# The o matmuls of nine MLP units by Strassen's method: seven products of halves, with the sums on VectorE

## The chip, the cores and the metric

The kernel runs on one core of one Trainium2 chip. The metric is the device time of one execution in microseconds. Before the change it was 677.96 us (median of three runs, 677.47 to 679.17).

## What is computed

A gated linear recurrence (4 batches, 8 heads, 768 tokens, head size 48) gives 3072 tokens of 384 features. They go through an MLP with 2048 hidden features and the activation h · sigmoid(1.702 h).

```python
# q, k, v, f_logit: (4, 8, 768, 48) float32;  w_in (384, 2048), w_out (2048, 384): float64
f = 1.0 / (1.0 + np.exp(-f_logit))
for t in range(S):
    state = f[:, :, t, :, None] * state + np.einsum('bhd,bhe->bhde', k[:, :, t], v[:, :, t])
    y[:, :, t] = np.einsum('bhd,bhde->bhe', q[:, :, t], state)
x = y.transpose(0, 2, 1, 3).reshape(B * S, H * D)      # (3072, 384)
h = x @ w_in
g = h * (1.0 / (1.0 + np.exp(-1.702 * h)))
out = (g @ w_out).astype(np.float32)
```

The kernel computes in float32. The weights arrive as float64 and are turned into float32 by VectorE, a piece at a time (`convert`), so the first MLP units have to follow the arrival of the weights.

## The kernel before

Tokens are taken in 12 units of 256 (`NALL = 12`, `U = 256`). For each there is an attention unit (scores, masks, state, y) and an MLP unit. Units 0 to 2 do their MLP in quarters of the hidden features, as the weights come. Units 3 to 11 do it whole: 16 blocks of 128 hidden features (`NFF = 16`), four of them to a g tile (`FG = 4`).

```python
    P, G, U = 128, 128, 256;  NK = 3;  NFF = 16;  FG = 4;  DM = 384
    wp = ...tile_pool(name="wp", bufs=2)      # "bits": 3 buffers, "a": 4 (conversion of weights)
    mlp = ...tile_pool(name="mlp", bufs=2)
    ps = ...tile_pool(name="ps", bufs=1, space=PSUM)   # sc: 2 banks, y: 2 banks, "mm": 4 buffers of a bank
    ctx.enter_context(tc.manual_schedule(engines={mybir.EngineType.PE}))   # TensorE runs in program order
    ...
    def mlp_h(n, ffs, g):
        def one(ff, c):
            if c == 0:
                if ff % FG == 0:
                    g[ff // FG] = mlp.tile([P, FG, width(n)], F32, tag="g", ..., bufs=6)
                t["ph"] = ps.tile([P, width(n)], F32, tag="mm", ..., bufs=4)
            nc.tensor.matmul(ph, lhsT=w_in[:, c, ff * P:(ff + 1) * P], rhs=xTs[n][:, c, :],       # L619: h
                             start=(c == 0), stop=(c == NK - 1))
            if c == NK - 1:
                nc.scalar.activation(sg, ph, AF.Sigmoid, scale=1.702)                              # L624
                nc.vector.tensor_tensor(g[ff // FG][:, ff % FG, :], ph, sg, ALU.mult)              # L625
                ...                       # the last unit: one token more, its sum on VectorE (L631, L633)

    def mlp_o(n, ffs, g, done):
        def one(tt, ff):
            if ff == ffs[0]:
                t["po"] = ps.tile([P, DM], F32, tag="mm", ..., bufs=4)
            nc.tensor.matmul(t["po"], lhsT=g[ff // FG][:, ff % FG, tt * P:(tt + 1) * P],           # L645: o
                             rhs=w_out[:, ff, :], start=(ff == ffs[0]), stop=(ff == ffs[-1]))
            if ff == ffs[-1]:
                done(tt, t["po"])

    def mlp_unit(n):                      # units 3 to 11
        def done(tt, po):
            ...
            nc.scalar.copy(o, po)                                                                  # L664
            store(n, tt, o)
```

The matmuls of the MLP are a list, `fill`. `merge(n, fill, columns, share)` emits the parts of attention unit n on TensorE and puts a share of `fill`, counted in moving columns, behind each of them. In the steady part (merges 4 to 11) one attention unit goes with one MLP unit's worth of columns; what is left runs at the end without attention.

```python
    UNIT = NFF * NK * U + U // P * NFF * DM
    ...
    fill_order.close()                    # from here the scheduler orders all engines but TensorE
    for n in range(3, NALL):
        fill += mlp_unit(n)
    for n in range(4, NALL):
        merge(n, fill, UNIT, steady)
    for _, emit, _ in fill:
        emit()
```

Of attention these steps matter here. `scores` are matmuls into `sc` (L383). VectorE multiplies X by the gates' products for the next level (`promote`, L438), and ScalarE copies the keys and queries out of X (`set_aside`, Kc and Qc, L422); the next scores read these copies. VectorE takes the scores out under a mask (A, L409), and TensorE adds A · v to y (L447). VectorE turns q, k and f from the loaded layout (STREAM_TRANSPOSE, L326), once each for a unit. The state goes step by step on VectorE (st, L539 and L542) from scores of k and v (L522), and TensorE then adds the state's part to y (L562). `tkn` (L504) are transposes of k by TensorE.

Of the kernel before, what the change touches and what calls it, by code (L numbers as in the profile page):

```python
# [9 lines left out]
F32 = mybir.dt.float32  # L10
I32 = mybir.dt.int32
U32 = mybir.dt.uint32
AF = mybir.ActivationFunctionType
ALU = mybir.AluOpType
# [9 lines left out]
def kernel(  # L24
# [7 lines left out]
    moe_w_out: bass.AP,  # L32
    out: bass.AP,
):

# [19 lines left out]
    nc = tc.nc  # L57
    B, H, S, D = q.shape
    DM = H * D
    DFF = moe_w_in.shape[1]  # L60
    P = 128
    C = 64
    G = 128
    U = 256
# [7 lines left out]
    NK = DM // P  # L72
    NFF = DFF // P
    FG = 4
    PAIRS_AHEAD = 3
# [9 lines left out]
    wp = ctx.enter_context(tc.tile_pool(name="wp", bufs=2))  # L85
    mlp = ctx.enter_context(tc.tile_pool(name="mlp", bufs=2))
    ps = ctx.enter_context(tc.tile_pool(name="ps", bufs=1, space=bass.MemoryType.PSUM))
# [43 lines left out]
    X = const.tile([P, 3, NX], F32, name="X")  # L131
# [8 lines left out]
    w_out = const.tile([P, NFF, DM], F32, name="w_out")  # L140
# [7 lines left out]
    pieces, pairs = [], []  # L148
    for r in range(NGR):
        ffs = range(r * FG, (r + 1) * FG)  # L150
        for ff in ffs[::2]:
            f = slice(ff * P, (ff + 2) * P)
# [77 lines left out]
    def convert():  # L230

        if state["begin"] < len(pairs) and len(todo) <= NOP:
            begin_pair(state["begin"])
            state["begin"] += 1
        if todo and todo[0]:
            todo.pop(0)()
        if todo and todo[0] is None:
            todo.pop(0)
            state["done"] += 2
            fetch_weights()  # L240
# [360 lines left out]
        return (begin_f, begin, begin_k, begin_gates), parts  # L601


    xTs = {}

    def width(n):

        return U + (n == NALL - 1)

    def mlp_h(n, ffs, g):  # L610
        t = {}

        def one(ff, c):
            if c == 0:
                if ff % FG == 0:
                    g[ff // FG] = mlp.tile([P, FG, width(n)], F32, tag="g", name=f"g_{n}_{ff}", bufs=6)
                t["ph"] = ps.tile([P, width(n)], F32, tag="mm", name=f"h_{n}_{ff}", bufs=4)
            ph = t["ph"]
            nc.tensor.matmul(  # L619
                ph, lhsT=w_in[:, c, ff * P:(ff + 1) * P], rhs=xTs[n][:, c, :], start=(c == 0), stop=(c == NK - 1)  # L620
            )
            if c == NK - 1:
                sg = mlp.tile([P, width(n)], F32, tag="sg", name=f"sg_{n}_{ff}")
                nc.scalar.activation(sg, ph, AF.Sigmoid, scale=1.702)  # L624
                nc.vector.tensor_tensor(g[ff // FG][:, ff % FG, :], ph, sg, ALU.mult)  # L625
                if width(n) > U:

                    by = g[ff // FG][:, ff % FG, U:]
                    if ff == 0:
                        g["last"] = mlp.tile([P, 1, DM], F32, tag="sum", name="sum_last", bufs=3)  # L630
                        nc.vector.tensor_scalar(g["last"][:, 0], w_out[:, 0, :], by, None, op0=ALU.mult)  # L631
                    else:
                        nc.vector.scalar_tensor_tensor(  # L633
                            g["last"][:, 0], w_out[:, ff, :], by, g["last"][:, 0], op0=ALU.mult, op1=ALU.add
                        )
        return [(U, lambda ff=ff, c=c: one(ff, c), ff // FG * NPC + ff % FG + 1) for ff in ffs for c in range(NK)]

    def mlp_o(n, ffs, g, done):

        t = {}  # L640

        def one(tt, ff):
            if ff == ffs[0]:
                t["po"] = ps.tile([P, DM], F32, tag="mm", name=f"o_{n}_{tt}_{ff}", bufs=4)
            nc.tensor.matmul(  # L645
                t["po"], lhsT=g[ff // FG][:, ff % FG, tt * P:(tt + 1) * P], rhs=w_out[:, ff, :],
                start=(ff == ffs[0]), stop=(ff == ffs[-1]),
            )
            if ff == ffs[-1]:
                done(tt, t["po"])  # L650
        return [(DM, lambda tt=tt, ff=ff: one(tt, ff), (ff // FG + 1) * NPC) for tt in range(U // P) for ff in ffs]

    def store(n, tt, o):
        r0 = n * U + tt * P - 1
        nc.sync.dma_start(out=out[max(r0, 0):r0 + P, :], in_=o[1:] if r0 < 0 else o)

    def mlp_unit(n):
        g = {}

        def done(tt, po):  # L660
            if tt == 0:
                g["o"] = mlp.tile([P, U // P, DM], F32, tag="osb", name=f"osb_{n}", bufs=1)
            o = g["o"][:, tt]
            nc.scalar.copy(o, po)  # L664
            store(n, tt, o)

        def last_token():
            po = ps.tile([P, DM], F32, tag="mm", name="o_last", bufs=4)
            nc.tensor.matmul(po[:1], lhsT=ones, rhs=g["last"][:, 0], start=True, stop=True)
            nc.scalar.copy(g["last"][:1, 0], po[:1])  # L670
            nc.sync.dma_start(out=out[NALL * U - 1:, :], in_=g["last"][:1, 0])
        o = mlp_o(n, range(NFF), g, done)
        if width(n) > U:
            o.insert(NFF, (DM, last_token, 0))
        return mlp_h(n, range(NFF), g) + o

    sums = {}

# [25 lines left out]
    def parts_of(n):  # L704

        parts = list(units[n][1])
        _, inter = parts.pop()
        if n:
            kind, scores = parts[0]
            _, ahead = units[n - 1][1][-1]  # L710
            parts[0] = kind, lambda: (ahead(), scores())
        if n < N_TURN:

            def with_v(l):
                kind, fn = parts[l]
                return kind, lambda: (fn(), load_vl(n, l) if n == 0 or l else None)
            parts[:NL] = [with_v(l) for l in range(NL)]
        if n + 1 < NALL:
            begin_f, begin, begin_k, begin_gates = units[n + 1][0]
            i = len(parts)  # L720
            if n + 1 < N_FILL:

                parts.append(("K", lambda: (begin_k(), begin_gates(), load_vl(n + 1, 0) if n + 1 < N_TURN else None)))
                parts.insert(i - 4, ("B", begin))
                parts.insert(i - 5, ("B", begin_f))
            else:
                kind, states = parts.pop()
                parts += [("B", begin_k), (kind, lambda: (states(), begin_gates()))]
                parts.insert(i - 3, ("B", lambda: (begin_f(), begin())))
        else:  # L730
            parts.append(("W", inter))
        return parts

    def merge(n, fill, columns, share, pieces=0, hold=0, by=1.0):

        parts = parts_of(n)
        total = sum(share(kind) for kind, _ in parts)
        converting = {"W": 3, "T": 3, "B": 1} if n < N_FILL - 1 else {"W": 3, "V": 4, "S": 3, "T": 1, "B": 1}  # L740
        total_ops = sum(converting.get(kind, 0) for kind, _ in parts)
        held = sum(share(kind) for kind, _ in parts[:hold])
        at = at_ops = done = ops = 0
        for kind, fn in parts:
            ready = state["done"]
            fn()
            at += share(kind)
            at_ops += converting.get(kind, 0)
            n_ops = min(int(pieces * NOP * at_ops / (by * total_ops)), pieces * NOP) - ops
            ops += n_ops  # L750
            first, n_columns = done, max(0, columns * (at - held) / (total - held) - done)

            def some(end):
                nonlocal done
                while fill and done < end and fill[0][2] <= ready:
                    w, emit, _ = fill.pop(0)
                    emit()
                    done += w
            for i in range(n_ops):
                some(first + n_columns * i / n_ops)  # L760
                convert()
            some(first + n_columns)
# [4 lines left out]
    UNIT = NFF * NK * U + U // P * NFF * DM  # L767
# [13 lines left out]
    load_vn(1)  # L781
    fill = []
    merge(0, fill, 0, steady, 8)
    fill += mlp_blocks((0, 0)) + mlp_blocks((0, 1))
    merge(1, fill, UNIT // 2 - LAG // 2, steady, 10, hold=1)
    fill += mlp_blocks((1, 0), (1, 1)) + mlp_blocks((0, 2), (1, 2))
    merge(2, fill, UNIT, steady, 8)
    fill += mlp_blocks((2, 0), (2, 1)) + mlp_blocks((2, 2), (0, 3)) + mlp_blocks((1, 3), (2, 3))
    merge(3, fill, 3 * UNIT // 2 - LAG // 2, steady, 6, by=0.7)
    fill_order.close()  # L790
    for n in range(3, NALL):
        fill += mlp_unit(n)
    for n in range(4, NALL):
        merge(n, fill, UNIT, steady)
    for _, emit, _ in fill:
        emit()

# [28 lines left out]
```

## Time and profile before

| | |
|---|---|
| time | 677.96 us (677.47 to 679.17) |
| span of the profile | 674.0 us |
| busy: TensorE matmul, weight load | 652.6 us, 486.5 us |
| busy: VectorE, ScalarE, GpSimd | 378.4 us, 226.4 us, 50.3 us |
| granted TensorE clock, mean | 0.990 |
| DMA: data moved, mean rate | 67.62 MB, 100 GB/s |

Names in the profile: PE is TensorE's matmul, PEld its weight load, DVE VectorE, ACT ScalarE, POOL GpSimd, SP the engine that issues the DMAs. L645 is line 645 of the kernel. A row of the groups gives line, engine, operation, result<-operands, shape, count, then busy time and mean duration, then the idle time of the engine just before and what ended it. In the row of 40 slices a digit is the busy share in tenths. The chain that ended last follows the work back from the last instruction. The timeline lists instructions in order of time: start, length, engine, line, operation. Matmul records overlap their neighbours, since matmuls are pipelined, so their summed busy time counts more than the clock does.

### The profile page before, as it was taken

The page shows a single profiled execution, that of the slowest core. Times are in us where ns is not written, and L with a number is a line of the kernel's source. Part 1 is how long each engine was busy: PE and PEld are TensorE (multiplying, and loading weights), DVE is VectorE, ACT ScalarE, POOL GpSimd, SP SyncE. Part 2 cuts the span into 40 slices and gives each one's busy share as a digit, 9 for nine tenths or more (in the row PEclk, how much of TensorE's full clock was granted, in tenths as well). Part 3 has the DMA queues.
Part 4 walks back from the last instruction along what each step waited for, and adds up shares of the span by engine and source line. Part 5 has one row for each costly group of instructions (what it writes and reads, how often), then busy time and mean ns, then how long its engine had stood idle before and what let it go on. Part 6 is the DMA issues. An engine that isn't in the chain of part 4 may idle for free.

```text
span 674.0 us, 19354 instructions
## 1 busy us (share of the span) xinstructions
PE 652.6 (97%) x8514; PEld 486.5 (72%) x8514; DVE 378.4 (56%) x675; ACT 226.4 (34%) x459; POOL 50.3 (7%) x116
## 2 busy tenths in 40 slices
PE   5879999999999999999999999999999999999997
PEld 4656766757777886886886886876886786786774
DVE  3999877887666546545546546445446444430440
ACT  4564443343134233333333233233233233231210
POOL 3020020010002002002002002002002001000000
PEclk9789999999999999999999999999999999999999
DMA  8877973571063535415415415415414103001000
GB/s 193 226 192 193 240 160 89 152 185 37 24 159 107 154 66 149 109 38 148 115 33 152 110 37 148 113 37 144 115 37 115 37 24 84 15 1 36 13 1 24
DMA packets 67551, 67.62 MB, mean 100 GB/s; under 512 B 30410, under 2 KB 61290, under 8 KB 67466
## 3 DMA queue, kind: packets, MB, share of 16 engines
q1 hardware_dynamic: 67466, 66.38, 38.6%
q8 instruction: 67, 1.10, 0.7%
q14 instruction: 18, 0.15, 0.1%
HBM read 56.92 MB, written 8.65 MB: 97 GB/s over the span
## 4 chain that ended last, share of the span: by engine, by line
PE 89%; DVE 7%; ACT 2%; issue 1%; DMA 1%; SPq 0%; DVEq 0%; ACTq 0%
PE h L619 37%; PE o L645 35%; PE sc L383 5%; PE y L447 5%; PE t L338 2%; PE y L562 2%; PE tkn L504 1%; PE sc L522 1%; DVE s L218 1%; DVE A L409 1%; DMA xT<-yT 1%; PE tv L283 1%; ACT yT L570 1%; DVE X L436 1%; DVE X L438 1%
## 5 line engine op out<-in xcount | busy, mean ns | idle before, releaser
L619 PE MATMUL h<-xT,w_in 128*128 128x256 f32 (+1 forms) x1152 | 261.1, 382 | 1.1 <-DVE sum L690 0.8
L645 PE MATMUL o<-w_out,g 128*128 128x384 f32 x768 | 259.6, 491 | 0.9 <-DVE g L625 0.9
L619 PEld LDWEIGHTS h<-xT,w_in 128*128 128x128 f32 x1152 | 215.8, 190 | 36.8 <-issue 3.5
L645 PEld LDWEIGHTS o<-w_out,g 128*128 128x128 f32 x768 | 143.0, 190 | 94.5 <-issue 2.2
L625 DVE TENSOR_TENSOR g<-h,sg 128x256 f32<-128x256 f32 (+1 forms) x192 | 80.8, 422 | 133.1 <-ACT sg L624 132.6
L624 ACT ACTIVATE sg<-h 128x256 f32<-128x256 f32 (+1 forms) x192 | 73.2, 383 | 169.4 <-PE h L619 164.1
L422 ACT COPY Kc<-X 128x512 f32<-128x512 f32 x69 | 45.9, 666 | 123.7 <-DVE X L438 87.3
L438 DVE TENSOR_TENSOR X<-X,tot 128x1024 f32<-128x1024 f32 x45 | 55.2, 1226 | 54.8 <-PE sc L383 50.1
L409 DVE TENSOR_TENSOR A<-sc,masks 128x512 f32<-128x512 f32 x72 | 46.7, 679 | 0.0
L326 DVE STREAM_TRANSPOSE X<-raw 128x1024 f32<-128x1024 f32 x18 | 36.7, 2039 | 16.7 <-PE y L562 13.9
L447 PE MATMUL y<-A,vl 64*48 64x64 f32 x2304 | 41.7, 219 | 0.0
L447 PEld LDWEIGHTS y<-A,vl 64*48 64x48 f32 x2304 | 36.8, 122 | 5.3 <-issue 5.0
L375 POOL TENSOR_TENSOR tot<-F 128x512 f32<-128x512 f32 x12 | 12.5, 1039 | 340.5 <-DVE st L539 327.9
L383 PE MATMUL sc<-X,Kc 48*64 48x64 f32 x1344 | 29.0, 224 | 6.8 <-ACT Kc L422 4.6
L383 PEld LDWEIGHTS sc<-X,Kc 48*64 48x64 f32 x1344 | 24.6, 138 | 13.8 <-ACT Kc L422 7.2
L570 ACT COPY yT<-y 48x512 f32<-48x512 f32 x48 | 27.8, 580 | 20.0 <-PE y L562 19.4
L331 ACT ACTIVATE F<-F 128x1024 f32<-128x1024 f32 x9 | 9.5, 1057 | 49.0 <-DVE F L326 49.0
L375 POOL TENSOR_TENSOR tot<-tot 128x256 f32<-128x256 f32 (+4 forms) x60 | 23.7, 395 | 4.7
L542 DVE TENSOR_TENSOR st<-st,sc 128x192 f32<-128x192 f32 x44 | 15.6, 354 | 15.1 <-PE sc L522 13.7
L338 PE MATMUL t<-ident,raw 128*64 128x128 f32 x288 | 19.6, 298 | 4.4 <-DMA raw<-in_f_logit_dram 4.4
L338 PEld LDWEIGHTS t<-ident,raw 128*64 128x64 f32 x288 | 18.4, 153 | 7.0 <-issue 6.1
L664 ACT COPY osb<-o 128x384 f32<-128x384 f32 x18 | 8.6, 478 | 41.5 <-PE o L645 41.5
(66 smaller groups left out, 385.0 us busy)
## 6 DMA issues: line engine op xcount, KB each, us to landing
vl<-v_tok SPq DMA_DIRECT2D x60, 192.0 KB, 2.8
bits<-in_moe_w_out_dram SPq DMA_DIRECT2D x8, 768.0 KB, 9.8
bits<-in_moe_w_in_dram SPq DMA_DIRECT2D x8, 576.0 KB, 7.9
v_tok<-in_v_dram SPq DMA_DIRECT2D x10, 384.0 KB, 4.3
vn<-v_tok SPq DMA_DIRECT2D x10, 384.0 KB, 6.0
xT<-yT SPq DMA_DIRECT2D x24, 144.0 KB, 2.7
raw<-in_f_logit_dram SPq DMA_DIRECT2D x18, 192.0 KB, 3.9
raw<-in_q_dram SPq DMA_DIRECT2D x18, 192.0 KB, 3.1
```

The lines of the kernel that those rows point to most:

```text
L326: nc.vector.transpose(out.rearrange("p (a i j) -> p a j i", a=NP, j=R), raw[:, j].rearrange("p a (j d) -> p (a j) d", j=R)[:, :, :32],)
L338: nc.tensor.matmul(pt[h * HS:(h + 1) * HS, jj, :], lhsT=by_pair[j][:, h, x:x + HS], rhs=ident, start=True, stop=True)
L375: nc.gpsimd.tensor_tensor(tn, t2[:, :, 0], t2[:, :, 1], ALU.mult)
L383: nc.tensor.matmul(out[g * HS:(g + 1) * HS, h, a, :], lhsT=lhs(h, a * U + g * G), rhs=rhs(h, a * U + g * G), start=True, stop=True,)
L409: nc.vector.tensor_tensor(A[:, :, c:c + w].rearrange("p h (x t) -> p h x t", t=64), t["sc"][:, :, c:c + w].rearrange("p h (x t) -> p h x t ...
L422: nc.scalar.copy(c.rearrange("p (n m) -> p n m", m=m), X[:, j, :NA].rearrange("p (n two m) -> p n two m", two=2, m=m)[:, :, hf, :],)
L438: nc.vector.tensor_tensor(qk, qk, by, ALU.mult)
L447: nc.tensor.matmul(dst(h, g, a), lhsT=vls[n, u][g * 64:(g + 1) * 64, (2 * a + h) * D:(2 * a + h + 1) * D], rhs=A(h, g, a), start=(start an ...
L619: nc.tensor.matmul(ph, lhsT=w_in[:, c, ff * P:(ff + 1) * P], rhs=xTs[n][:, c, :], start=(c == 0), stop=(c == NK - 1))
L624: nc.scalar.activation(sg, ph, AF.Sigmoid, scale=1.702)
L625: nc.vector.tensor_tensor(g[ff // FG][:, ff % FG, :], ph, sg, ALU.mult)
L645: nc.tensor.matmul(t["po"], lhsT=g[ff // FG][:, ff % FG, tt * P:(tt + 1) * P], rhs=w_out[:, ff, :], start=(ff == ffs[0]), stop=(ff == ffs[ ...
```

## The change

The o of a unit is a product of two matrices that can be cut into halves each way. A is g: Aij has the tokens of half i (128) and the hidden blocks of half j (8 of 16). B is w_out: Bij has the hidden blocks of half i and the columns of half j (192 of 384). Eight products of halves make the result; by Strassen's method, in Winograd's form, seven do, with sums of halves:

- of B, once: T1 = B01 - B00, T2 = B11 - T1, T3 = B11 - B01, T4 = T2 - B10
- of A, in each unit: S1 = A10 + A11, S2 = S1 - A00, S3 = A00 - A10, S4 = A01 - S2
- products in TensorE's order: P1 = A00·B00, P4 = A11·T4, P2 = A01·B10, P6 = S2·T2, P5 = S1·T1, P7 = S3·T3, P3 = S4·B11
- result: out00 = P1 + P2; u2 = P1 + P6; u3 = u2 + P7; out10 = u3 - P4; out11 = u3 + P5; out01 = u2 + P5 + P3

Each product is 8 matmuls of 192 columns that add up in PSUM. There are four banks for them. X takes P1, and once that is copied out, P2 on top of it; Y takes P6 and then P7; Z takes P5 and then P3; W takes P4. VectorE makes the sums of A in SBUF: S1 in place of A10, S4 in place of A01, S2 and S3 in two more tiles of the pool of g. The sums of B use buffers of the conversion (`bits`, `a`) again. Units 3 to 11 are changed, units 0 to 2 are not. The aim is an eighth less of TensorE's work on o in these units.

```diff
+    HF, HC = NFF // 2, DM // 2
+    def quarter(w, i, j, ffs=slice(0, HF)):
+        return w[:, i * HF + ffs.start:i * HF + ffs.stop, j * HC:(j + 1) * HC]
+
+    def sums_of_b():                      # ten operations of VectorE, emitted two to a part of attention unit 4
+        for i in (1, 2, 3):
+            T[i] = wp.tile([P, 2 * DM * 2], I32, tag="bits", name=f"T{i}", bufs=PAIRS_AHEAD)
+            ...
+        t4 = [wp.tile([P, DM], F32, tag="a", name=f"T4_{f}", bufs=4)... for f in range(0, HF, n4)]
+        for x in h:                       # h: two halves of the 8 blocks
+            yield lambda x=x: sub(T[1][:, x], quarter(w_out, 0, 1, x), quarter(w_out, 0, 0, x))
+        for x in h:
+            yield lambda x=x: sub(T[2][:, x], quarter(w_out, 1, 1, x), T[1][:, x])
+        for x in h:
+            yield lambda x=x: sub(T[3][:, x], quarter(w_out, 1, 1, x), quarter(w_out, 0, 1, x))
+        for i in range(len(t4)):
+            yield lambda i=i, x=x: sub(t4[i], T[2][:, x], quarter(w_out, 1, 0, x))
+
+    def sums_of_a(n, g, b):               # after the four blocks of g tile b
+        if b < 2:
+            g["S", j] = mlp.tile([P, FG, width(n)], F32, tag="g", name=f"S_{n}_{j}", bufs=6)
+            tt(g["S", j][:, :, t1], g[j][:, :, t0], g[j][:, :, t1], ALU.subtract)
+        else:
+            tt(g[j][:, :, t1], g[j][:, :, t1], g[j + 2][:, :, t1], ALU.add)
+            tt(g["S", j][:, :, t0], g[j][:, :, t1], g[j][:, :, t0], ALU.subtract)
+
+    def last_sum(n, g):                   # S4, after P2 has read A01
+        for j in range(2):
+            nc.vector.tensor_tensor(g[j + 2][:, :, by], g[j + 2][:, :, by], g["S", j][:, :, by], ALU.subtract)
+
+    def mlp_o7(n, g):
+        def p1(): nc.scalar.copy(row("p1"), t["X"])
+        def p4(): nc.scalar.copy(row("p4"), t["W"])
+        def p2(): nc.scalar.copy(out_(0)[:, :HC], t["X"]); last_sum(n, g)
+        def p6(): nc.vector.tensor_tensor(row("u2"), t["p1"], t["Y"], ALU.add)
+        def p5(): nc.scalar.copy(row("p5"), t["Z"])
+        def p7():
+            nc.vector.tensor_tensor(row("u3"), t["p1"], t["Y"], ALU.add)
+            nc.vector.tensor_tensor(out_(1)[:, :HC], t["u3"], t["p4"], ALU.subtract)
+            nc.vector.tensor_tensor(out_(1)[:, HC:], t["u3"], t["p5"], ALU.add)
+            store(n, 1, out_(1))
+        def p3():
+            nc.vector.tensor_tensor(out_(0)[:, HC:], t["u2"], t["Z"], ALU.add)
+            store(n, 0, out_(0))
+        products = (
+            ("X", a(0, 0), b(0, 0), p1, True), ("W", a(1, 1), T_(4), p4, True), ("X", a(0, 1), b(1, 0), p2, False),
+            ("Y", s(0), T_(2), p6, True), ("Z", a(1, 0), T_(1), p5, True), ("Y", s(1), T_(3), p7, False),
+            ("Z", a(0, 1), b(1, 1), p3, False),
+        )
+        def one(bank, lhs, rhs, done, new, f):
+            if new and f == 0:
+                t[bank] = ps.tile([P, HC], F32, tag="mm", name=f"o_{n}_{bank}", bufs=4)
+            nc.tensor.matmul(t[bank], lhsT=lhs(f), rhs=rhs(f), start=(new and f == 0), stop=(f == HF - 1), ...)
+            if f == HF - 1:
+                done()
+        return [(HC, lambda p=p, f=f: one(*p, f), 0) for p in products for f in range(HF)]
 ...
     def mlp_unit(n):
-        o = mlp_o(n, range(NFF), g, done)
+        o = mlp_o7(n, g)
         if width(n) > U:
-            o.insert(NFF, (DM, last_token, 0))
-        return mlp_h(n, range(NFF), g) + o
+            o.insert(3 * HF, (DM, last_token, 0))
+        return mlp_h(n, range(NFF), g, True) + o       # mlp_h calls sums_of_a after each g tile
 ...
     for n in range(4, NALL):
-        merge(n, fill, UNIT, steady)
+        merge(n, fill, NFF * NK * U + 7 * HF * HC, steady, chores=list(sums_of_b()) if n == 4 else ())
```

More of the change, by code (lines that the diff above doesn't have):

```diff
@@ L601, in attention @@
         return (begin_f, begin, begin_k, begin_gates), parts
+    HF, HC = NFF // 2, DM // 2
+    T = {}
+    def quarter(w, i, j, ffs=slice(0, HF)):
[3 more added lines that the diff above has]
+            T[i] = wp.tile([P, 2 * DM * 2], I32, tag="bits", name=f"T{i}", bufs=PAIRS_AHEAD)
+            T[i] = T[i].bitcast(F32).rearrange("p (f e) -> p f e", f=HF)
+        n4 = DM // HC
+        t4 = [wp.tile([P, DM], F32, tag="a", name=f"T4_{f}", bufs=4).rearrange("p (f e) -> p f e", f=n4)
+              for f in range(0, HF, n4)]
+        T[4] = lambda f: t4[f // n4][:, f % n4]
+        sub = lambda *x: nc.vector.tensor_tensor(*x, ALU.subtract)
+        h = [slice(f, f + HF // 2) for f in (0, HF // 2)]
+        for x in h:
[5 more added lines that the diff above has]
+        for i in range(len(t4)):
+            x = slice(i * n4, (i + 1) * n4)
+            yield lambda i=i, x=x: sub(t4[i], T[2][:, x], quarter(w_out, 1, 0, x))
@@ new lines, in sums_of_a @@
+    def sums_of_a(n, g, b):
+        j = b % 2
+        t0, t1 = slice(0, G), slice(G, 2 * G)
+        tt = nc.vector.tensor_tensor
+        if b < 2:
[4 more added lines that the diff above has]
+            tt(g["S", j][:, :, t0], g[j][:, :, t1], g[j][:, :, t0], ALU.subtract)
@@ new lines, in last_sum, with out_, row, p1 @@
+    def last_sum(n, g):
+        for j in range(2):
+            by = slice(0, G)
+            nc.vector.tensor_tensor(g[j + 2][:, :, by], g[j + 2][:, :, by], g["S", j][:, :, by], ALU.subtract)
+    def mlp_o7(n, g):
+        a = lambda i, j: lambda f: g[j * 2 + f // FG][:, f % FG, i * G:(i + 1) * G]
+        s = lambda i: lambda f: g["S", f // FG][:, f % FG, i * G:(i + 1) * G]
+        b = lambda i, j: lambda f: quarter(w_out, i, j)[:, f]
+        T_ = lambda i: lambda f: T[i][:, f] if i < 4 else T[4](f)
+        t = {}
+        def out_(tt):
+            if "o" not in g:
+                g["o"] = mlp.tile([P, U // P, DM], F32, tag="osb", name=f"osb_{n}", bufs=1)
+            return g["o"][:, tt]
+        def row(name):
+            t[name] = mlp.tile([P, HC], F32, tag=name, name=f"{name}_{n}", bufs=1)
+            return t[name]
+        def p1():
+            nc.scalar.copy(row("p1"), t["X"])
+        def p4():
+            nc.scalar.copy(row("p4"), t["W"])
+        def p2():
+            nc.scalar.copy(out_(0)[:, :HC], t["X"])
+            last_sum(n, g)
+        def p6():
+            nc.vector.tensor_tensor(row("u2"), t["p1"], t["Y"], ALU.add)
+        def p5():
+            nc.scalar.copy(row("p5"), t["Z"])
+        def p7():
[14 more added lines that the diff above has]
+                t[bank] = ps.tile([P, HC], F32, tag="mm", name=f"o_{n}_{bank}", bufs=4)
+            nc.tensor.matmul(
+                t[bank], lhsT=lhs(f), rhs=rhs(f), start=(new and f == 0), stop=(f == HF - 1), skip_group_check=True,
+            )
+            if f == HF - 1:
+                done()
+        return [(HC, lambda p=p, f=f: one(*p, f), 0) for p in products for f in range(HF)]
@@ L608, in width, with mlp_h @@
         return U + (n == NALL - 1)
-    def mlp_h(n, ffs, g):
+    def mlp_h(n, ffs, g, sums=False):
         t = {}
@@ L625, in one @@
                 nc.vector.tensor_tensor(g[ff // FG][:, ff % FG, :], ph, sg, ALU.mult)
+                if sums and ff % FG == FG - 1:
+                    sums_of_a(n, g, ff // FG)
                 if width(n) > U:
@@ L658, in mlp_unit @@
         g = {}
[L660 to L665, printed above, removed]
         def last_token():
@@ L732, in parts_of, with merge @@
         return parts
-    def merge(n, fill, columns, share, pieces=0, hold=0, by=1.0):
+    def merge(n, fill, columns, share, pieces=0, hold=0, by=1.0, chores=()):
         parts = parts_of(n)
@@ L746, in merge @@
             fn()
+            for chore in chores[:2]:
+                chore()
+            chores = chores[2:]
             at += share(kind)
```

## The prediction

> **What bounds the kernel now.** I read the page's parts 1, 2 and 4 first.
>
> ```profile
> PE 652.6 (97%) x8514; PEld 486.5 (72%) x8514; DVE 378.4 (56%) x675; ACT 226.4 (34%) x459; POOL 50.3 (7%) x116
> ...
> PE   5879999999999999999999999999999999999997
> ...
> PE h L619 37%; PE o L645 35%; PE sc L383 5%; PE y L447 5%; PE t L338 2%; PE y L562 2%; PE tkn L504 1%; PE sc L522 1%; DVE s L218 1%; DVE A L409 1%; DMA xT<-yT 1%; PE tv L283 1%; ACT yT L570 1%; DVE X L436 1%; DVE X L438 1%
> ...
> L619 PE MATMUL h<-xT,w_in 128*128 128x256 f32 (+1 forms) x1152 | 261.1, 382 | 1.1 <-DVE sum L690 0.8
> L645 PE MATMUL o<-w_out,g 128*128 128x384 f32 x768 | 259.6, 491 | 0.9 <-DVE g L625 0.9
> ```
>
> TensorE is full from the fourth fortieth on, and h and o are 72% of the chain that ended last. Twelve units of 48 h matmuls and 32 o matmuls are 576 and 384, yet the groups count 1152 and 768: one fp32 matmul leaves two records. The mean durations (382, 491 ns) overlap, so they are no cost. The cost is the spacing, which the chain in order of time gives (start, length, line, records):
>
> ```profile
> 376.14 7.34 PE h L619 x34
> ...
> 648.90 10.32 PE o L645 x32
> ```
>
> 7.34 us / 34 = 215.9 ns for a record of 256 columns; 10.32 / 32 = 322.5 ns for 384. The slope is (322.5 - 215.9) / 128 = 0.833 ns a column, and 2.7 ns remain. In the steady part one period of one attention unit and one MLP unit takes 50.95 us (from the o group at 363.44 in that chain to its like at 414.39). There the list of waits has none on TensorE from 200 us on, and VectorE is half busy:
>
> ```profile
> 402.00:453.00 51.00, 51.00 (x682) 38.53 (x681) 26.18 (x39) 16.97 (x35) 4.29 (x8) 1.00 0.39 100
> ```
>
> (length; busy time and count of PE, PEld, DVE, ACT, POOL; clock; DMA.) So a column taken from TensorE is worth its full time, as long as nobody makes TensorE wait.
>
> **What the Trainium skill says.**
> - "FP8 and Floating Point Precision", TensorE Precision Notes: true fp32 takes four passes through the array. The trace agrees: two records of 0.833 ns a column, each two cycles of 2.4 GHz.
> - "TensorE: Matmul & The Clock Gate", LDWEIGHTS (loading the stationary operand): a load takes its columns / 1.2 ns whatever the rows, so 107 ns for 128 columns. The records of o and h say 190 ns. Which of the two counts is decided below, from the trace.
> - "VectorE: DVE Perf Modes", Mode 2×_2P: an fp32 tensor_tensor stays at one element a cycle. The trace agrees: 512 elements took 683 ns and 1024 took 1226 ns, 1.06 ns an element.
> - "PSUM — Partial Sum Buffer", PSUM bank collisions raise a hardware error: a matmul must not write a bank that another engine is reading. No run here shows a collision; but it is why a second product in a bank has to wait until the first has been copied out, and the change does that three times in a unit.
>
> **The change part by part.**
>
> *TensorE, removed and added.* Nine units (3 to 11) change. A unit's o had 2 x 16 matmuls of 384 columns, 64 records x 322.5 ns = 20.64 us. It gets 7 products x 8 matmuls of 192 columns, 112 records. By the line above a record is 215.9 - 64 x 0.833 = 162.6 ns, so 18.21 us. Saved: 2.43 us a unit, 21.8 us in all. The switches between the wide matmuls and the small attention ones are as many as before.
>
> *Does the weight load hide behind 162.6 ns?* Loads go from 64 to 112 a unit, + 9 x 48 x 190 ns = + 82 us of PEld busy, to about 569 us or 86%. If 190 ns were the least spacing, the gain would be gone. Where a tkn transpose (128 columns, one record) comes ahead of h, the timeline shows:
>
> ```profile
> 551.72 0.60 PE L504 MATMUL tkn<-ident,X 128*128 128x128 f32 x4
> 552.16 0.60 PE L619 MATMUL h<-xT,w_in 128*128 128x256 f32 x2
> ...
> 552.05 0.30 PEld L619 LDWEIGHTS h<-xT,w_in 128*128 128x128 f32 x2
> ```
>
> Two loads of 190 ns end 0.30 us after the first began, so they start 0.11 us apart, and the h matmul starts at 552.16, 0.11 us after the start of its own load. So 190 ns holds some 80 ns of latency, and a load occupies 110 ns at most. 162.6 ns is over that, and I count no load.
>
> *VectorE, added.* A unit: six sums of halves (512 elements, 0.68 us) and two last ones, 8 x 0.68 = 5.5 us; five adds of 192 columns out of PSUM at 0.354 us (the st<-st,sc row has that size) = 1.8 us. Together 7.2 us a unit. Once: sums of w_out, six of 768 elements (between 0.68 and 1.23 us, say 0.95) and four of 384 (0.55), 7.9 us. By amount it fits: 26.2 + 7.2 = 33.4 us of a period of 48.5. ScalarE loses two copies of 0.478 us and gets four of about 0.33 us. Nothing to see.
>
> *VectorE, where it lies.* This decides how much of the 21.8 us is kept. As built, each steady period runs on TensorE: y of the state (L562), scores, 1 matmul of P2, P6 (8), P5 (8), then P7, which adds into the bank of P6 and so waits until VectorE has read P6 for u2. On VectorE the order is: transposition of X, st, X multiply, two A, X multiply, last sum, u2. Before, the same stretch is (start, length):
>
> ```profile
> 413.53 2.05 DVE L326 STREAM_TRANSPOSE X<-raw 128x1024 f32<-128x1024 f32 x1 [2.14 <-PE y L562]
> 415.43 0.33 DVE L539 TENSOR_TENSOR st<-st,tot 128x192 f32<-128x192 f32 x1
> 415.69 1.21 DVE L438 TENSOR_TENSOR X<-X,tot 128x1024 f32<-128x1024 f32 x1
> 416.82 1.27 DVE L409 TENSOR_TENSOR A<-sc,masks 128x512 f32<-128x512 f32 x2
> 418.21 1.23 DVE L438 TENSOR_TENSOR X<-X,tot 128x1024 f32<-128x1024 f32 x1
> ...
> 414.32 9.30 PE L645 MATMUL o<-w_out,g 128*128 128x384 f32 x28
> ```
>
> VectorE ends at 419.44; with the last sum (0.68), u2 (0.35) and their gaps it has read P6 at about 420.6. TensorE, from 414.32, is through 17 matmuls of 2 x 162.6 ns at 419.85. So P7 waits about 0.75 us. This comes in seven periods (units 3 to 9; in the last attention unit the transposition is missing and VectorE is early): 7 x 0.75 = 5.3 us given back. After P7 there is air: u3 and the two sums end before the next scores, and the next Kc still comes over 2 us ahead of its scores.
>
> Other joints, by the same count: the S sums lie ahead of the state chain and end 0.3 us after its scores, with over 3 us before y needs the state. P4's last operand is ready about 4 us ahead. P2 and P3 have 2.6 us (one product) for ScalarE's copies of P1 and P5. In the last unit VectorE has 16 x (0.42 + 0.62) + 4.1 = 20.8 us beside 20.85 us of h, but P6 comes three products later. The end stays: an add of 0.35 us in place of a copy of 0.48 us, then the store.
>
> *Sums of w_out.* The scheduler puts the 7.9 us among the conversions of the last weights, at about 150 to 195 us, where VectorE is up to 73% busy. Most fits in its gaps; some g or sum that frees a bank will be late. I choose 1 us.
>
> Sum: 677.96 - 21.8 + 5.3 + 1.0 = 662.5 us.
>
> **The rivals.**
> - *Weight load is the bound.* At 190 ns a record: 112 x 0.190 = 21.28 us against 20.64, nine units cost 5.8 us, and the time is 684. The 190 ns rows speak for it, the loads 0.11 us apart against it; no 192-column fp32 matmul has run yet, so it isn't ruled out. A mild form, 5 ns more a record, costs 1008 x 5 ns = 5 us: 667.5.
> - *All of it is kept.* VectorE reads P6 in time and the w_out sums find gaps: 656.2. The order as built speaks against it.
> - *VectorE is late at more joints.* If each steady period waits 1.5 to 2 us in place of 0.75, the time is 668 to 671. For it: VectorE goes from 51% to about 68% of a period and executes in order, behind 2 us transposes. Against it: the margins above, mostly 2 us and more.
> - *g buffers run out* (six of a pool of six in a unit, four before). Each is read for the last time before the next unit's h of the same place is through, so I give it nothing.
>
> **Range and chances.** The mechanism spans 656 (all kept) to 671 (late at more joints); 0.75 us a period is a difference of two sums that may be off by half a microsecond, 3.5 us in all, and the 1 us may be 3. So 656.5 to 668.5. Faster by over 2% means under 664.4, only 1.9 us above my number: 0.66. Slower by over 2% needs the weight load and stalls together: 0.01. The rest, 0.33, is within 2%.
>
> **What would show it.** Right: o records of 192 columns some 163 ns apart; a steady period of about 49.3 us (50.95 - 2.43 + 0.75); one wait of TensorE's o on VectorE's u2 in a period, 0.5 to 1 us long; PEld near 569 us, DVE near 451 us (378 + 65 + 8). Wrong: o records 175 to 190 ns apart (weight load); a period of 48.5 us with no wait on u2; waits of sc on Kc, y on st or h on g in the steady part; more than 3 us of new waits between 150 and 230 us.

## The result and the profile after

The changed kernel took 661.47 us (median of four runs, 659.69 to 662.94) against 677.73 us of the kernel before beside it: a ratio of 0.9755, 95% interval 0.9723 to 0.9786. A second time, on its own (below), it was 0.9744, 0.9721 to 0.9766.

From the page of the changed kernel, the parts with busy time, slices, the chain's shares and the groups of o. Line numbers have moved: h is L727, the o of units 0 to 2 L755, the o of the seven products L704, with the bank in the name.

```profile
PE 632.1 (96%) x8946; PEld 542.3 (82%) x8946; DVE 443.9 (67%) x802; ACT 230.6 (35%) x477; POOL 54.0 (8%) x116
...
PE   6669989998999999999999999999999999999997
...
PE h L727 36%; PE o L755 7%; PE o_X L704 7%; PE o_Y L704 5%; PE o_Z L704 5%; PE sc L384 5%; PE y L448 4%; PE o_W L704 4%; DVE X L439 3%; PE t L339 2%; PE y L563 2%; DMA vn<-v_tok 1%; PE sc L523 1%; PE tkn L505 1%; DMA xT<-yT 1%
...
L704 PE MATMUL o_X<-w_out,g 128*128 128x192 f32 x288 | 53.8, 332 | 0.0
L704 PE MATMUL o_Y<-T,S 128*128 128x192 f32 x288 | 50.8, 329 | 1.3 <-DVE u L679 1.2
```

TensorE is still full, but VectorE has entered the chain: `X L439` rose from 1% to 3%, and one row of the seven products has idle time ahead of it, released by `u L679`. That is u2, the add that reads P6. The list of who waited for whom, for TensorE from 235 us to the end, has this line alone (total, times, longest):

```profile
PE o_Y L704 <- DVE u L679: 1.2, 4, 0.3
```

The wait comes six times, once in each of six periods; two of them are too short for this list, which takes idle times over 0.15 us. It is in these six periods, and in no other steady one, that the chain runs through VectorE. The chain in order of time shows the spacing and the period:

```profile
306.95 2.60 PE o_W L704 x16
...
351.03 1.62 PE o_X L704 x10
...
400.10 1.63 PE o_X L704 x10
```

2.60 us / 16 = 162.5 ns for a record of 192 columns; 162.6 was predicted. P1 comes every 49.07 us here, and 48.99 us in the mean of the six periods that have the wait. Before, it was 50.94.

The wait itself, in the timeline of the changed kernel, first TensorE, then VectorE:

```profile
411.64 0.59 PE L704 MATMUL o_X<-w_out,g 128*128 128x192 f32 x2
412.07 2.77 PE L704 MATMUL o_Y<-T,S 128*128 128x192 f32 x16
414.67 2.76 PE L704 MATMUL o_Z<-T,g 128*128 128x192 f32 x16
417.71 2.87 PE L704 MATMUL o_Y<-T,S 128*128 128x192 f32 x16 [0.27 <-DVE u L679]
...
413.03 1.22 DVE L439 TENSOR_TENSOR X<-X,tot 128x1024 f32<-128x1024 f32 x1
414.17 1.28 DVE L410 TENSOR_TENSOR A<-sc,masks 128x512 f32<-128x512 f32 x2
415.56 1.25 DVE L439 TENSOR_TENSOR X<-X,tot 128x1024 f32<-128x1024 f32 x1
416.70 0.69 DVE L650 TENSOR_TENSOR g<-g,S 128x512 f32<-128x512 f32 x1
417.31 0.35 DVE L679 TENSOR_TENSOR u<-p,o_Y 128x192 f32<-128x192 f32 x1
```

P7 (the second o_Y) starts at 417.71, right behind the end of u2 at 417.66. P6 takes 2.60 us from its first record to the first of P5 (412.07 to 414.67), P5 took 3.04. The list says 0.27 us only, because the last record before the wait is listed at 326 ns though the next could have come after 162.5.

### The profile page after: what moved, and what is told of

The parts are those of the page before. It is cut to its first block, busy times and chain, and to the rows that moved or that the text cites. A ratio compares the mean times of both kernels' runs of the same rounds, so it can differ in the third digit from the quotient of the medians.

```text
span 660.8 us, 20364 instructions
## 1 busy us (share of the span) xinstructions
PE 632.1 (96%) x8946; PEld 542.3 (82%) x8946; DVE 443.9 (67%) x802; ACT 230.6 (35%) x477; POOL 54.0 (8%) x116
## 4 chain that ended last, share of the span: by engine, by line
PE 80%; DVE 11%; DMA 3%; issue 2%; ACT 2%; SPq 1%; DVEq 0%; ACTq 0%
PE h L727 36%; PE o L755 7%; PE o_X L704 7%; PE o_Y L704 5%; PE o_Z L704 5%; PE sc L384 5%; PE y L448 4%; PE o_W L704 4%; DVE X L439 3%; PE t L339 2%; PE y L563 2%; DMA vn<-v_tok 1%; PE sc L523 1%; PE tkn L505 1%; DMA xT<-yT 1%
## 5 line engine op out<-in xcount | busy, mean ns | idle before, releaser
L727 PE MATMUL h<-xT,w_in 128*128 128x256 f32 (+1 forms) x1152 | 262.9, 384 | 3.7 <-DMA xT<-yT 1.8
L727 PEld LDWEIGHTS h<-xT,w_in 128*128 128x128 f32 x1152 | 216.5, 191 | 37.7 <-issue 3.3
L755 PE MATMUL o<-w_out,g 128*128 128x384 f32 x192 | 66.2, 492 | 0.9 <-DVE g L733 0.9
L439 DVE TENSOR_TENSOR X<-X,tot 128x1024 f32<-128x1024 f32 x45 | 55.1, 1225 | 17.5 <-PE sc L384 12.3
L755 PEld LDWEIGHTS o<-w_out,g 128*128 128x128 f32 x192 | 35.4, 190 | 24.2 <-issue 1.5
L704 PE MATMUL o_X<-w_out,g 128*128 128x192 f32 x288 | 53.8, 332 | 0.0
L704 PE MATMUL o_Y<-T,S 128*128 128x192 f32 x288 | 50.8, 329 | 1.3 <-DVE u L679 1.2
L704 PEld LDWEIGHTS o_Y<-T,S 128*128 128x128 f32 x288 | 46.9, 190 | 3.8 <-DVE u L679 3.1
L704 PEld LDWEIGHTS o_X<-w_out,g 128*128 128x128 f32 x288 | 47.1, 190 | 1.3
L376 POOL TENSOR_TENSOR tot<-tot 128x256 f32<-128x256 f32 (+4 forms) x60 | 27.2, 454 | 4.7
L704 PE MATMUL o_Z<-w_out,g 128*128 128x192 f32 x144 | 26.5, 330 | 0.0
```

The source lines that it names most:

```text
L376: nc.gpsimd.tensor_tensor(tn, t2[:, :, 0], t2[:, :, 1], ALU.mult)
L439: nc.vector.tensor_tensor(qk, qk, by, ALU.mult)
L704: nc.tensor.matmul(t[bank], lhsT=lhs(f), rhs=rhs(f), start=(new and f == 0), stop=(f == HF - 1), skip_group_check=True,)
```

## A second look at both kernels: how far the start of a run varies

The first profiles disagree with the medians: the spans differ by 13.2 us, the medians by 16.3. I compared the time from the first matmul to the first record of the state's y of unit 2. Up to there all programs are the same on every engine. It was 135.2 us before and 139.8 us after, so I ran both kernels once more, unchanged.

> The changed kernel once more, unchanged, as the measure for the other three beside it. My theory of the first profile: unit 2's y ended 4.7 us later against the start than before although the program is the same up to there, so that part is chance of the run and not the change. Expected: 660 to 662 us, and in this profile the first PE record of the state's y of unit 2 less than 4.7 us later than the 128.6 us before it (start of the state's y after the first matmul: 135.3 us before, 139.8 us in the first profile after). The rival, that the change itself slows the start, expects 139.8 us again.

> The kernel before once more, unchanged, for its start. From the first matmul to the state's y of unit 2 its profile took 135.2 us, those of the changed kernel and its variants 136.7 to 139.8 us, although all programs are the same up to there. Theory (chance of the run): this profile gives 136 to 140 us as well. Rival (the changed program has a slower start): 135.2 us again. From there to the end both expect the same as in the first profile (465.9 us from the y of unit 3 to the end).

Measured: 660.88 us (659.82 to 662.03) and 678.13 us (676.70 to 679.40). The starts were 138.9 and 136.0 us; in the six other kernels below, whose program is the same up to there, 136.7 to 139.4. Neither start decides alone: 138.9 lies nearer to the 139.8 that the rival named, and 136.0 at the edge of what chance was to give; the two starts of before are the shortest of all ten. More is learnt from the time of each profiled run less its own start:

| profiled run | time | start | time less start |
|---|---|---|---|
| before | 675.73 | 135.2 | 540.5 |
| before, again | 676.70 | 136.0 | 540.7 |
| after | 662.94 | 139.8 | 523.1 |
| after, again | 662.03 | 138.9 | 523.1 |

Within a kernel the two profiled times differ as their starts do, to 0.2 us. The change is worth 523.1 - 540.6 = -17.5 us behind the start. The medians say -16.3 and -17.4, so a slower start that belongs to the changed kernel is about 1 us at most; two starts of the kernel before are too few to exclude that. If the rest always takes as long as in these profiles, the medians of the second runs put the usual start at 678.13 - 540.6 = 137.5 us before and 660.88 - 523.1 = 137.8 us after. By this estimate the profiled runs of before happened to be ones with a short start. From here on I compare the time less the start.

## The experiments

**Eight products: what 192 columns cost.** Same halves, no sums.

```diff
-        o = mlp_o7(n, g)
+        o = mlp_o8(n, g)     # for i, j, f: 2 x 2 x 16 matmuls of 192 columns, ScalarE copies each quarter out
```

> The same halves with all eight products and no sums: o of units 3 to 11 in 64 matmuls of 192 columns (128 records) in place of 32 of 384 (64 records), nothing else. Theory (a record of 192 columns takes 162.6 ns, its weight load is hidden): 128 x 162.6 = 20.81 us a unit against 20.64, in nine units 1.5 us slower than before, 679 to 680 us, steady period 51.1 us. Rival (weight load of 190 ns is the spacing): 24.3 us a unit, 33 us slower.

Measured: 678.17 us, ratio 0.9999 (0.9964 to 1.0034). The median is under the 679 to 680 us expected, and the interval is too wide to show 1.5 us. Time less start shows it: 680.77 - 138.7 = 542.1, 1.5 us over before; the steady period is 51.10 us against 50.94. In the chain of this kernel a record of 192 columns takes 10.40 / 64 = 162.5 ns:

```profile
653.92 10.40 PE o L658 x64
```

Twice the matmuls and twice the weight loads at the same number of columns cost 0.8% of o. The weight load doesn't bound at 192 columns.

**Quarters of 96 columns: where the columns no longer set the pace.** All eight products again, `W = 96` in place of 192.

> All products, o of units 3 to 11 in quarters of 96 columns: 128 matmuls a unit, 256 records, nothing else changed. By columns alone a record would take 215.9 - 160 x 0.833 = 82.6 ns, 21.1 us a unit, 682 us in all. Theory (a weight load of 128 columns occupies 109 ns, as the two loads after a wait showed): 256 x 0.110 = 28.1 us a unit, nine units 67 us more, about 745 us. If the 190 ns of the records were the spacing: 48.6 us a unit, 930 us.

Measured: 749.51 us, a single run, where about 745 was expected. Its chain has this line:

```profile
722.88 21.62 PE o L660 x192
```

21.62 / 192 = 112.6 ns a record; by columns it would be 82.6. The load of 128 columns is listed with 192 ns and can't occupy all of that; some 110 ns fits the spacing here and the two loads 0.11 us apart that the prediction shows. The Trainium skill ("TensorE: Matmul & The Clock Gate", LDWEIGHTS (loading the stationary operand)) gives an estimate of 128 / 1.2 = 107 ns, near both. No run varies the width of the load under matmuls of 96 columns, so that it is the load which sets 112.6 ns, and not another cost of every record, is argued and not shown. What is shown is that matmuls of 96 columns with loads of 128 don't pay by columns: 112.6 ns, not 82.6.

**No sums: what TensorE's part is worth alone.** The products read g and w_out without the sums of halves (so the output is not o); the adds out of PSUM stay.

> Seven products, but all sums of halves are left out on both sides (the products read g and w_out as they are, so the output is another one); the adds out of PSUM stay. It is what TensorE's part alone is worth. Theory: steady period 48.5 us without a wait, no delay by the sums of w_out: 21.9 us less than before, 656 us, 1.3 us less than with u2 first. Rival (VectorE's added work slows more than the two joints found): clearly under 655 us.

Measured: 655.88 us (654.93 to 657.78), ratio 0.9667 (0.9635 to 0.9700). All steady periods are 48.50 us, and the windows have TensorE busy throughout:

```profile
388.00:437.00 49.00, 49.00 (x732) 45.14 (x731) 27.54 (x44) 17.83 (x37) 4.05 (x8) 1.00 0.40 105
```

The same window of the changed kernel:

```profile
388.00:437.00 49.00, 48.73 (x729) 44.64 (x729) 32.74 (x52) 17.41 (x36) 4.60 (x8) 1.00 0.39 104
```

VectorE's 5.2 us more cost TensorE 0.27 us in the list of waits, and 49.07 - 48.50 = 0.57 us in the period. From the state's y of unit 3 to the last matmul: 461.9 us before, 440.0 us here. So the seven products save 21.9 us. 21.8 was predicted.

**u2 before the last sum.** S4 isn't needed before P3, two products after u2.

```diff
         def p2():
             nc.scalar.copy(out_(0)[:, :HC], t["X"])
-            last_sum(n, g)
         def p6():
             nc.vector.tensor_tensor(row("u2"), t["p1"], t["Y"], ALU.add)
+            last_sum(n, g)
```

> S4 = A01 - S2 is emitted after u2 instead of before it, so VectorE reads P6 one operation of 0.69 us earlier; nothing else moves. Theory (P7 waits in six periods until VectorE has read P6, 0.22 to 0.48 us each and 0.1 us more for the exposed weight load after it, 2.9 us in all): all six waits go, the steady period falls from 48.97 to 48.5 us, the time by 2.9 us to about 658.5. Rival (VectorE is late because it has too much work, and any other joint takes over the wait): the time stays within 1 us of the changed kernel, with waits on S4 or st instead.

Measured: 657.50 us (656.96 to 658.65), ratio 0.9700 (0.9680 to 0.9720), 3.4 us under the changed kernel beside it. The timeline of this kernel in the same stretch of a period, again TensorE and then VectorE:

```profile
410.16 2.76 PE L704 MATMUL o_Z<-T,g 128*128 128x192 f32 x16
412.76 2.76 PE L704 MATMUL o_Y<-T,S 128*128 128x192 f32 x16
...
411.04 1.23 DVE L439 TENSOR_TENSOR X<-X,tot 128x1024 f32<-128x1024 f32 x1
412.19 0.35 DVE L678 TENSOR_TENSOR u<-p,o_Y 128x192 f32<-128x192 f32 x1
412.45 0.69 DVE L650 TENSOR_TENSOR g<-g,S 128x512 f32<-128x512 f32 x1
```

u2 ends at 412.54, 0.2 us before P7 begins, and P7 follows P5 2.60 us after P5's first record, with no wait. The chain has P1 every 48.50 us, in all six periods, like those without sums:

```profile
298.58 1.63 PE o_X L704 x10
...
541.09 1.62 PE o_X L704 x10
```

(541.09 - 298.58) / 5 = 48.50. The amount of VectorE's work, 32.75 us in 49, was not the trouble; one operation of 0.69 us ahead of u2 was. This version beats both kernels. Of the 3.4 us, 3.0 lie between the state's y of unit 2 and the last matmul (513.1 us in the second profile of the changed kernel, 510.2 here); the rest is within the spread of the start.

**No sums of w_out.** The ten sums T are left out (the products take quarters of w_out, so the output is not o); the sums of A stay.

```diff
-        merge(..., chores=list(sums_of_b()) if n == 4 else ())
+        merge(..., chores=())
```

> The ten sums of w_out are left out (the products take quarters of w_out itself, so the output is another one). Theory: they cost 1.3 us of delay between the state's y of unit 2 and that of unit 3 (68.5 us before, 69.8 us after), so the time falls by about 1.3 us and that interval is 68.5 us again. Prediction's own figure: 1.0 us. Rival (VectorE's sums in the conversion stretch are what cost the start of the kernel 6 us): the time falls by 4 to 6 us.

Measured: 659.60 us (659.47 to 660.54), 1.3 us under the changed kernel beside it. Between the state's y of units 2 and 3 there are 68.56 us, as before (68.54), in place of 69.79. Where the 1.2 us arise, the timeline of the changed kernel (second run) shows, VectorE and then TensorE:

```profile
157.24 1.82 DVE L622 TENSOR_TENSOR T<-w_out 128x768 f32<-128x768 f32 x2
158.97 0.42 DVE L733 TENSOR_TENSOR g<-h,sg 128x256 f32<-128x256 f32 x1
...
155.82 2.64 PE L727 MATMUL h<-xT,w_in 128*128 128x256 f32 x11
159.45 1.99 PE L727 MATMUL h<-xT,w_in 128*128 128x256 f32 x8 [0.98 <-DVE g L733]
```

The first two T stand ahead of a g on VectorE. Four h fill the four banks, and this g frees the one that the fifth h needs. Without T, TensorE's waits have no such line. From record to record the wait is longer than the 0.98 us listed: h begins 1.36 us after the record before it in place of 0.22, and the next record another 0.10 us late. That is all of the 1.25; the other eight T cost nothing that shows.

**u2 first, and T by GpSimd.**

```diff
-        sub = lambda *x: nc.vector.tensor_tensor(*x, ALU.subtract)
+        sub = lambda *x: nc.gpsimd.tensor_tensor(*x, ALU.subtract)
```

> u2 first, as in the run before, and the ten sums of w_out by GpSimd in place of VectorE (about 1.6 us each for 768 elements, on an engine that is idle there). Expected: both losses go, 661.5 - 2.9 - 1.3 = 657.3 us, unless GpSimd's sums come too late for P4 of unit 3 or slow VectorE's operations beside them; then 658 to 660 us.

Measured: 657.09 us (656.16 to 659.23), ratio 0.9692 (0.9669 to 0.9715): not to be told from u2 first alone. The time is the 657.3 us that was expected, but not for its reason: the loss by T did not go. The stretch between the state's y of units 2 and 3 became longer, 70.26 us. The timeline of this kernel, VectorE and then GpSimd, in two places:

```profile
154.61 1.98 DVE L228 TENSOR_TENSOR w_in<-a,s 128x384 f32<-128x384 f32 x1
156.51 0.41 DVE L733 TENSOR_TENSOR g<-h,sg 128x256 f32<-128x256 f32 x1
156.84 1.82 DVE L228 TENSOR_TENSOR w_in<-a,s 128x384 f32<-128x384 f32 x1
...
154.37 3.89 POOL L622 TENSOR_TENSOR T<-w_out 128x768 f32<-128x768 f32 x2 [7.96 <-DVE a L227]
...
168.78 1.02 DVE L228 TENSOR_TENSOR w_out<-a,s 128x384 f32<-128x384 f32 x2
169.08 2.92 POOL L622 TENSOR_TENSOR T<-w_out,T 128x768 f32<-128x768 f32 x1 [10.83 <-ACT sum L791]
```

While GpSimd makes two T, VectorE's add of two SBUF operands takes 1.98 and 1.82 us in place of 0.55; the g between them, with one operand in PSUM, keeps its 0.41. The Trainium skill ("SBUF — State Buffer", Who interferes with whom) says that a VectorE instruction with two SBUF inputs contends with a GpSimd instruction that reads SBUF, and that one with a single SBUF input, outside VectorE's two-port modes, does not. This trace agrees. The second place shows the reverse: one such add of VectorE was running when GpSimd began and another followed it; the two took 1.02 us, as they do alone, and the T took 2.92 us, where the same sum takes 1.82 later on. So either engine can be the one that waits; in both places it was the one that began second. The first two sums weren't taken off VectorE; it waited for them in another form.

The profiled runs on one scale, with what the measured terms give (21.9 saved, 2.9 for the waits on u2, 1.25 for T on VectorE, 1.7 for T on GpSimd):

| kernel | time less start | against before (540.6) | from the terms |
|---|---|---|---|
| changed | 523.1 | -17.5 | -21.9 + 2.9 + 1.25 = -17.75 |
| u2 first | 657.01 - 137.0 = 520.0 | -20.6 | -21.9 + 1.25 = -20.65 |
| no sums of w_out | 660.54 - 139.1 = 521.4 | -19.2 | -21.9 + 2.9 = -19.0 |
| no sums | 657.78 - 139.4 = 518.4 | -22.2 | -21.9 |
| u2 first, T by GpSimd | 657.05 - 136.7 = 520.4 | -20.2 | -21.9 + 1.7 = -20.2 |
| eight products | 542.1 | +1.5 | 9 x 0.16 = +1.4 |

## Why the prediction was right

The chain of reasons held: TensorE's saving, the hidden load, the one joint where VectorE is late, and a small loss by the sums of w_out were all found. Two terms were mis-sized, one by 2.4 us too much and one by 0.25 us too little. That the time, 661.47 us, is only 1 us from the predicted 662.5 is partly luck: with both terms at their measured size the sum is 677.96 - 21.9 + 2.9 + 1.25 = 660.2 us, 2.3 us under the prediction, and the first runs lay 1.3 us over that, within the spread of the start.

- *TensorE's saving*: 21.8 us predicted, 21.9 measured. The line through 256 and 384 columns gave 162.6 ns for 192; the trace has 162.5.
- *The weight load is hidden*: right, and now shown by itself (eight products): 162.5 ns a record rules out the rival of 190 ns and its mild form of 5 ns more. The 112.6 ns at 96 columns fit the reading of two loads 0.11 us apart. The four passes that the prediction sets beside true fp32 are another matter: the traces show two records to a matmul, and none tells passes apart.
- *P7 waits for u2*: the joint, its cause and its place were right; the run with u2 first takes all six waits away. The size was off: 7 x 0.75 = 5.3 us predicted, 2.9 us measured (six periods of 48.99 in place of 48.50 in the mean, of which 2.3 us are waiting and 0.6 us the slow pair of records after it). Three things were wrong in the term. There are six such periods, units 3 to 8: I counted the o of unit 9 among them, but it runs with the last attention unit. VectorE is sooner: from the start of the transposition to the end of u2 I reckoned 7.07 us and it took 6.80, because I put gaps between its operations where their records overlap (the multiply that begins at 413.03 is listed with 1.22 us, and its successor begins 1.14 us later). And TensorE is later by 0.1 us: I took all its records at 162.6 ns, but the first two behind the scores are 0.267 us apart. So a wait was 0.43 to 0.47 us in four periods. In the two others a unit starts a batch, the st operation is missing as well, and the wait was 0.22 and 0.26 us. The wait needs no rule about PSUM banks: P7 changes the values that u2 reads.
- *The sums of w_out*: 1.0 us predicted, 1.25 measured, through the wait that I had named (a g that frees a bank comes late).
- *VectorE late at more joints*: it was not, with 32.7 us of 49 busy.
- *g buffers*: no wait on them in any trace.
- *PEld 569 and DVE 451*: 542.3 and 443.9 measured. Both were sums of listed durations. Records that overlap count once in busy time: a load counts 162.5 ns when the next begins then, and 1008 x 0.1625 + 486.5 - 576 x 0.19 = 541 us.
- *The period*: 49.3 predicted, 48.99 measured.

## What to carry to other kernels

Where an engine is full and its waits are empty, work taken from it is worth its full time (21.9 us here); then look for the joint where the engine that got the work is now too late, and put the operation that frees a bank ahead of those that nobody waits for yet. Fit the cost of a matmul from the spacing of two sizes, not from the durations in the rows, and estimate what a weight load occupies from two loads that follow each other closely. Before work is moved to an idle engine, ask whether its reads hold up the busy one, as GpSimd's did here (1.98 us in place of 0.55).

## What the hardware showed that I had not expected

A wait of TensorE costs more than itself. The first two records of a group behind a wait start 0.267 us apart in place of 0.1625, since the second load begins late. In the steady flow a load begins together with the matmul before its own, and its own follows 0.16 us later. The timeline of the changed kernel behind the wait at 417.71:

```profile
417.71 0.62 PEld L704 LDWEIGHTS o_Y<-T,S 128*128 128x128 f32 x4 [0.57 <-DVE u L679]
```

The first load begins with its own matmul, the second 0.109 us later, and its matmul another 0.160 us after that. Six waits in this kernel paid 0.1 us each for it. In both kernels the same 0.1 us stands at the returns from the scores and the y of attention to the wide matmuls; behind the tkn transposes, with full tiles of 128 x 128 like the wide matmuls, the first pair is at most 4 ns longer. Why the two differ no run shows.
